# Where in 256 bytes the split operands of a fused attention and feed-forward kernel begin: one place per chunk for x, one per slot for the squares

## The chip, the cores and the metric

The kernel runs on one core of a Trainium2 chip, as one program. The metric is the device time of the whole program in microseconds, smaller is better. The time before is 639.32 us, the median of three runs (634.35, 640.18 and 639.32 us); one more execution was taken with the hardware profiler and lasted 636.35 us, of which the span from the first to the last instruction is 634.6 us.

## The reference, cut to what matters

Attention over 4 batches, 8 heads, 768 positions and 64 values per head: each query sees the keys less than 16 positions away, and 24 summaries of blocks of 32 (the maximum of the keys, the mean of the values). The result, 3072 tokens of 512 values, goes through a feed-forward layer with squared ReLU.

```python
    k_sum = k.reshape(B, H, nb, block, D).max(axis=3)
    v_sum = v.reshape(B, H, nb, block, D).mean(axis=3)
    scores_all = np.concatenate([scores_l_m, scores_s], axis=-1)   # window, then summaries
    a = np.exp(scores_all - max); a = a / (a.sum() + 1e-09)
    x = np.matmul(a, v_all)                       # -> (3072, 512)
    h = np.maximum(x @ w_in, 0.0)                 # 512 -> 2048
    return h * h @ w_out                          # 2048 -> 512
```

## The kernel before, in words

**Numbers.** Everything that TensorE multiplies in the feed-forward layer is split into a high part and a low part of four bytes per value (type fp32r): x into `xh` and `xl`, the weights into two halves of `w_sb[f]`, the squares into `gh` and `gl`. Each product is then three matmuls: high by high, high by low, low by high.

**Chunks, blocks and slots.** The 3072 tokens are 12 chunks of 256 (`c`), the 2048 hidden values are 16 blocks of 128 (`f`). The first layer, `ffn1` (L391, matmuls at L395), makes one block of one chunk from 12 matmuls: for each of four parts of the 512 inputs, the stationary operand is 128x128 of `w_sb[f]`, and the moving operand is 256 columns (1024 bytes per partition) of `xh` or `xl`. The second layer, `ffn2` (L429, matmuls at L436), makes for each of the two halves of the chunk three matmuls with a stationary 128x128 piece of `gh` or `gl` and a moving operand of 512 columns of `w_sb[f]`. A slot (L470) handles two blocks: 24 matmuls of the first layer, then 12 matmuls of the second layer for the two blocks of the slot before, and then ScalarE and VectorE make this slot's squares (`squares`, L420: ReLU at L403, high square L409, exact square L414, low part L417). In the text, F1 is the group of 24 matmuls and F2 the group of 12; a chunk is eight slots, so eight times F1 and F2.

**The order.** The first two chunks and the attention ahead of them (groups 0 to 5) are written out by hand in the string `START` (L43), because the weights arrive and are split there. From chunk 2 on (L641) the slots run in order, and `period` (L487) hangs the attention of later groups between them: in the eighth slot's place stand `outputs` (L354, matmuls at L364), `scores_by_group` (L269, matmuls at L281) and `split_x` (L384), which writes `xh` (L379, ScalarE) and `xl` (L382, VectorE) of the next chunk. The program's order is the one written; no planner changes it.

**Places.** All tiles of interest are in the SBUF, each partition's bytes one after the other. In the built program the weights' rooms (pool `big`, 8192 bytes each) all begin at byte 160 of a 256-byte line of addresses, and so do the buffers of x and of the squares. All pieces of the weights that a matmul reads begin at multiples of 512 bytes in their room, all pieces of x at multiples of 512 behind the first byte of the chunk's x. So the difference between where x begins and where the weights begin, taken in 256 bytes, is just the number that the list `begin_x` (L110) gives for that chunk: one number for `xh`, one for `xl`. In this document "place" is this number, taken in 256. `x_buf` has two buffers for each of `xh` and `xl`, each with 128 values to spare, and `x_part` (L374) takes buffer `c % 2` from `begin_x[c]` on. Chunks 0 to 11 have the places 0, 0, 0, 64, 128, 192, 256 (which is 0), 32, then (`xh`, `xl`) = (0, 64), (0, 128), (0, 256), and 320 (which is 64). The squares `gh_sb` and `gl_sb` (L113, L114) are one tile each, of four blocks of 1024 bytes; a slot uses two of them, the next slot the other two. Their place is always 0.

Of the kernel before, what the change touches and what calls it, by code (L numbers as in the profile page):

```python
# [12 lines left out]
F32R = mybir.dt.float32r  # L13
# [11 lines left out]
P = 128  # L25
NT = S // P
NPAIR = H // 2
TPC = 2
CT = TPC * P
# [44 lines left out]
def attn_ffn_kernel(ctx: ExitStack, tc: tile.TileContext, q, k, k0, kt, v, vt, v0, w, masks, gmasks, ident, mean, out):  # L74
# [3 lines left out]
    const = ctx.enter_context(tc.tile_pool(name="const", bufs=1))  # L78
# [28 lines left out]
    ksum = const.tile([P, NPAIR, NB], F32, name="ksum")  # L107
    vsum = const.tile([P, NPAIR, 32], F32, name="vsum")

    begin_x = [(0, 0), (0, 0), (0, 0), (64, 64), (128, 128), (192, 192), (256, 256), (32, 32), (0, 64), (0, 128), (0, 256), (320, 320)]  # L110
    x_buf = {n: [const.tile([P, NPAIR * CT + 128], F32R, name=f"{n}{i}") for i in range(2)] for n in ("xh", "xl")}
    r_sb = const.tile([P, 2, CT], F32, name="r")
    gh_sb = const.tile([P, 4, CT], F32R, name="gh")  # L113
    gl_sb = const.tile([P, 4, CT], F32R, name="gl")  # L114


    bank = [ps_s.tile([P, DM], F32, name=n, tag=f"{n}{i}") for i, n in enumerate(["s_ps"] * 4 + ["ph"] * 2)]
# [26 lines left out]
    def sum_v0(vn):  # L144


        ps = ps_o.tile([P, DM], F32, name="o_ps")
        for t in range(NT):
            o = 20 - 4 * t
            for j in range(4):  # L150
                nc.tensor.matmul(
                    ps[j * 32 : j * 32 + 32, 0:P], lhsT=mean_sb[:, o : o + 32],
                    rhs=vn[t // 3][:, t % 3, j * P : (j + 1) * P], start=(t == 0), stop=(t == NT - 1),
                )
        return ps

    def place_v0(ps, j, eng):
        for g in range(2):
            copy(
                eng, v_sb[g][96:128, :, j * P : (j + 1) * P],  # L160
                ps[j * 32 : j * 32 + 32, 0:P].unsqueeze(1).to_broadcast([32, 2, P]),
            )
# [18 lines left out]
    def sum_k(b, p):  # L181
        nc.vector.tensor_reduce(
            out=ksum[:, p], in_=kv[b, p][:, 0:S].rearrange("a (n j) -> a n j", j=BLOCK), op=ALU.max, axis=AX.X
        )

    def sum_v(b, p):
        nc.vector.tensor_reduce(
            out=vsum[:, p, 0:NB], in_=kv[b, p][:, S : 2 * S].rearrange("a (n j) -> a n j", j=BLOCK), op=ALU.add, axis=AX.X
        )
        nc.vector.tensor_scalar_mul(vsum[:, p, 0:NB], vsum[:, p, 0:NB], 1.0 / BLOCK)  # L190

    def place_k(g):
        dst = by_run(g)[:, 4] if g < FROM_GROUPS else by_pair(g)[:, :, :, 64:GK]
        nc.vector.tensor_copy(out=dst, in_=ksum.unsqueeze(1).to_broadcast([P, 2, NPAIR, NB]))
# [58 lines left out]
    xh, xl = {}, {}  # L253
# [60 lines left out]
    def exponentials(g, h):  # L314
        half, i = divmod(h, 4)
        e = e_sb[:, h, 0 : NK if g < FROM_GROUPS else GK]
        nc.scalar.activation(e, e, AF.Exp, bias=nmx[half][:, i : i + 1], scale=-1.0, accum_out=sm[half][:, i : i + 1])  # L317
# [7 lines left out]
    def inverse(half):  # L325
        nc.vector.tensor_scalar_add(sm[half], sm[half], 1.0e-9)  # L326
        nc.vector.reciprocal(sm[half], sm[half])  # L327
        del nmx[half]
# [49 lines left out]
    def high_x(g):  # L378
        nc.scalar.copy(out=x_part(xh, "xh", g), in_=x_ps[g])  # L379
# [11 lines left out]
    def ffn1(c, f, ph):  # L391
        n = 0
        for cc in range(NC4):
            for w, x in ((0, xh), (1, xh), (0, xl)):
                nc.tensor.matmul(  # L395
                    ph, lhsT=w_sb[f][:, w, cc * P : (cc + 1) * P], rhs=x[c][:, cc, :], start=(n == 0), stop=(n == 3 * NC4 - 1)
                )
                n += 1
        return ph

    def relu(ph, r, eng):
        if eng is nc.scalar:
            nc.scalar.activation(r, ph, AF.Relu)  # L403
        else:
            eng.tensor_scalar_max(r, ph, 0.0)  # L405
        return r

    def high_square(gh, r):
        nc.scalar.activation(gh, r, AF.Square)  # L409
        return gh  # L410

    def square(ph, r):

        nc.vector.tensor_mul(out=ph, in0=ph, in1=r)  # L414

    def low_square(gl, ph, gh):
        nc.vector.tensor_sub(out=gl, in0=ph, in1=gh.bitcast(F32))  # L417
        return gl

    def squares(ph, k):  # L420

        r = relu(ph, r_sb.rearrange("p a b -> p (a b)"), nc.scalar)
        gh, gl = (b[:, 2 * k : 2 * k + 2, :].rearrange("p a b -> p (a b)") for b in (gh_sb, gl_sb))
        high_square(gh, r)
        square(ph, r)
        low_square(gl, ph, gh)
        return [(gh_sb[:, 2 * k + i, :], gl_sb[:, 2 * k + i, :]) for i in range(2)]

    def ffn2(c, f, gh, gl, first, last):  # L429
        if first:  # L430
# [11 lines left out]
    def evict(c, f, tt, eng):  # L442

        if (c, tt) in parked:
            ob = parked[c, tt]
            nc.vector.tensor_add(out=ob, in0=o_ps[c][tt], in1=ob)
        else:
            ob = work.tile([P, DM], F32, name="ob", tag="ob", bufs=4)
            copy(eng, ob, o_ps[c][tt])
        if f < NF - 1:  # L450
            parked[c, tt] = ob
        else:
            r0 = c * CT + tt * P
            nc.sync.dma_start(out=out[r0 : r0 + P, :], in_=ob)
# [7 lines left out]
    def finish():  # L462

        for p in behind:
            ffn2(*p)
        done = [p[:2] for p in behind if p[-1]]
        behind.clear()
        return done[0] if done else None

    def slot(c, f, before, after, last):  # L470

        ph = bank[4 + f // 2 % 2]
        for i in range(2):
            ffn1(c, f + i, ph[:, i * CT : (i + 1) * CT])
        done = finish()
        for do in before:
            do()
        for i, g_ in enumerate(squares(ph, f // 2 % 2)):
            behind.append((c, f + i, *g_, f + i == 0, f + i == NF - 1))
        for tt in range(2 if done else 0):  # L480
            evict(*done, tt, nc.scalar)
        for do in after:
            do()
        for do in last:
            do()
# [45 lines left out]
    vn, tp, ph_of, r_of, g_of, v_mean = {}, {}, {}, {}, {}, {}  # L531
# [30 lines left out]
    def begin(op, i, j, eng):  # L562


        if op == "KS":
            sum_k(0, i)
        elif op == "PK":
            place_k(i)
        elif op == "SV":
            v_mean[0] = sum_v0([vn[0], vn[1]])  # L570
        elif op == "VC":
            place_v0(v_mean[0], i, eng)
        elif op == "KT":
            sum_k(1, i)
        elif op == "VT":
            sum_v(1, i)

        elif op == "S":
            if i < FROM_GROUPS:
                (scores_kt if i < FROM_KT else scores)(i, 2 * j, 2 * j + 2)  # L580
            else:
                scores_by_group(i)
        elif op == "TT":
            mask_max(i, j)
        elif op == "E":
            exponentials(i, j)
        elif op == "NR":
            inverse(j)
        elif op == "N":
            norm(i, j, eng)  # L590
        elif op == "T":
            held["T", i, j] = free.pop(0)
            tp[i, j] = turn_pe(i, j, bank[held["T", i, j]])
        elif op == "TC":
            copy(eng, pT[i % 2][:, j * 4 : j * 4 + 4], tp.pop((i, j)))
            free.append(held.pop(("T", i, j)))
        elif op == "O":
            outputs(i)
        elif op == "XH":
            high_x(i)  # L600
        elif op == "XL":
            low_x(i)

        elif op in ("HI", "LO", "SH", "AD", "CA", "SU"):
            {"HI": sign_w, "LO": round_w, "SH": shift_w, "AD": add_w, "CA": high_w, "SU": low_w}[op](i, eng)

        elif op == "F1":
            held["F1", i] = free.pop(0)
            ph_of[i] = ffn1(*units[i][:2], bank[held["F1", i]][:, 0:CT])
        elif op == "RE":  # L610
            r_of[i] = relu(ph_of[i], r_sb[:, i % 2, :], eng)
        elif op == "SQ":
            g_of[i] = [high_square(gh_sb[:, i % 4, :], r_of[i])]
        elif op == "MU":
            square(ph_of[i], r_of[i])
        elif op == "GL":
            g_of[i].append(low_square(gl_sb[:, i % 4, :], ph_of.pop(i), g_of[i][0]))
            free.append(held.pop(("F1", i)))
        elif op == "F2":
            c, f, f0, f1 = units[i]  # L620
            ffn2(c, f, *g_of.pop(i), f == f0, f == f1 - 1)
        elif op == "EV":
            evict(*units[[4, 15, 26, 31][i]][:2], j, eng)
        else:
            raise AssertionError(op)

    with tc.manual_schedule(engines=None):
        for token in START.split():
            what, i, j, eng = re.fullmatch(r"(L:[a-z]+|F[12]|[A-Z]+)\.?(\d*)\.?(\d*)([avp]?)", token).groups()
            i, j = int(i or 0), int(j or 0)  # L630
# [10 lines left out]
        for c in range(2, n_c):  # L641
            for f in range(0, NF, 2):
                n = (f + 2) // 2 % 8
# [85 lines left out]
```

## Time and profile before

| what | value |
|---|---|
| median of three runs | 639.32 us |
| the profiled execution | 636.35 us |
| its span | 634.6 us |
| mean granted TensorE clock | 0.989 |
| TensorE matmul busy | 605.5 us, 95% |
| TensorE weight load busy | 546.8 us, 86% |
| VectorE, ScalarE, GpSimd busy | 386.1, 262.7 and 88.3 us |
| chain that ended last: matmuls of L395 and of L436 | 44% and 41% |

The chain of work that ended last is followed back from the last instruction; each of its rows has the start, the length, the engine, what it writes, the line and the number of instructions. A matmul's own duration in the profile (283 ns for 256 columns) is longer than the step from one matmul's start to the next, since matmuls are pipelined. What counts for the time is the step; it is the length of a row of the chain divided by its count.

### The profile page before, as it was taken

How to read it: one execution, taken by the hardware profiler on the slowest of the kernel's cores; microseconds unless marked ns; L12 is line 12 of the kernel's file. 1: busy time of each engine (PE TensorE's matmuls, PEld its weight loads, DVE VectorE, ACT ScalarE, POOL GpSimd, SP SyncE). 2: the span in 40 equal slices, each digit the busy share in tenths (PEclk: the TensorE clock that was granted, in tenths of full speed). 3: DMA queues.
4: the chain of work that ended last, by engine and by line, in shares of the span. 5: the costliest groups of instructions: out<-in, count | busy, mean ns of one | idle time of the engine just before them, and what ended most of it. 6: DMA issues, size and time to landing. Idle time of an engine off the chain costs nothing.

```text
span 634.6 us, 14142 instructions
## 1 busy us (share of the span) xinstructions
PE 605.5 (95%) x5792; PEld 546.8 (86%) x5792; DVE 386.1 (61%) x1077; ACT 262.7 (41%) x690; POOL 88.3 (14%) x83
## 2 busy tenths in 40 slices
PE   3699999999989999999999998999999999999997
PEld 2488889989979989999989987998998998998996
DVE  4889989768535755756644772683763663653221
ACT  3678887232424324424424423333424333332222
POOL 2565662002000000002000000000200000000000
PEclk9879999999999999999999998999999999999999
DMA  9999611553043134124016106205005001000000
GB/s 302 364 344 323 210 62 52 165 171 81 1 110 110 48 86 132 51 70 99 1 53 165 51 26 159 84 1 135 35 1 135 34 0 52 34 2 1 34 1 33
DMA packets 55105, 60.56 MB, mean 95 GB/s; under 512 B 40321, under 2 KB 40449, under 8 KB 52993
## 3 DMA queue, kind: packets, MB, share of 16 engines
q1 hardware_dynamic: 55040, 59.67, 31.5%
q8 instruction: 45, 0.74, 0.5%
q14 instruction: 20, 0.16, 0.1%
HBM read 53.36 MB, written 6.29 MB: 94 GB/s over the span
## 4 chain that ended last, share of the span: by engine, by line
PE 93%; DMA 3%; DVE 2%; issue 1%; SPq 0%; ACT 0%; DVEq 0%
PE ph L395 41%; PE o_ps L436 41%; PE ph L364 3%; PE s_ps L395 3%; PE s_ps L281 2%; DMA q_sb<-in_q 2%; PE s_ps L296 1%; DMA mask_sb<-in_masks 1%; DVE e_sb L309 1%; PE s_ps L364 1%; PE ph L339 1%; PE s_ps L264 0%; DVE sm L326 0%; SPq L174 0%; DVE w_raw L239 0%
## 5 line engine op out<-in xcount | busy, mean ns | idle before, releaser
L395 PE MATMUL ph<-xh,w_sb 128*128 128x256 f32 x1448 | 265.3, 283 | 2.6 <-issue 2.1
L395 PEld LDWEIGHTS ph<-xh,w_sb 128*128 128x128 f32 x1448 | 230.0, 191 | 10.8 <-issue 2.6
L436 PE MATMUL o_ps<-w_sb,gh 128*128 128x512 f32 x768 | 238.8, 392 | 0.0
L395 PE MATMUL ph<-xl,w_sb 128*128 128x256 f32 x724 | 204.5, 282 | 0.0
L414 DVE TENSOR_TENSOR ph<-ph,r 128x512 f32<-128x512 f32 (+1 forms) x101 | 64.8, 643 | 162.8 <-ACT r L403 162.1
L436 PEld LDWEIGHTS o_ps<-w_sb,gh 128*128 128x128 f32 x768 | 137.6, 188 | 23.8 <-issue 0.2
L436 PE MATMUL o_ps<-w_sb,gl 128*128 128x512 f32 x384 | 150.0, 390 | 0.8 <-DVE gl L417 0.8
L403 ACT ACTIVATE r<-ph 128x512 f32<-128x512 f32 (+1 forms) x91 | 51.8, 569 | 228.8 <-PE ph L395 223.3
L395 PEld LDWEIGHTS ph<-xl,w_sb 128*128 128x128 f32 x724 | 138.1, 191 | 0.0
L317 ACT ACTIVATE e_sb<-e_sb,nmx 128x88 f32<-128x88 f32 (+1 forms) x192 | 69.8, 365 | 69.9 <-DVE nmx L309 69.9
L350 DVE STREAM_TRANSPOSE pT<-e_sb 32x256 f32<-32x256 f32 x216 | 94.1, 435 | 3.4 <-POOL e_sb L333 0.4
L436 PEld LDWEIGHTS o_ps<-w_sb,gl 128*128 128x128 f32 x384 | 72.1, 188 | 17.3 <-DVE gl L417 1.3
L333 POOL TENSOR_TENSOR e_sb<-e_sb,sm 128x352 f32<-128x352 f32 (+1 forms) x43 | 34.6, 808 | 337.5 <-DVE sm L327 200.5
L417 DVE TENSOR_TENSOR gl<-ph,gh 128x512 fp32r<-128x512 f32 (+1 forms) x101 | 64.3, 636 | 10.6 <-DVE ph L414 0.5
L409 ACT ACTIVATE gh<-r 128x512 fp32r<-128x512 f32 (+1 forms) x112 | 63.9, 571 | 8.7 <-DVE r L405 5.2
L243 POOL TENSOR_TENSOR w_raw<-w_raw 128x1024 int32<-128x1024 int32 x16 | 35.2, 2210 | 27.2 <-DVE w_raw L239 10.1
L317 ACT ACTIVATION_READ_ACCUMULATOR e_sb<-e_sb,nmx 128x1 f32 x192 | 36.1, 188 | 0.0
L309 DVE CUSTOM_DVE_ANT_0 e_sb<-s_ps,gmask_sb 128x88 f32<-128x88 f32 x144 | 27.1, 245 | 0.4
L382 DVE TENSOR_TENSOR xl<-ph,xh 128x512 fp32r<-128x512 f32 x19 | 13.1, 691 | 22.7 <-ACT xh L379 22.7
L326 DVE TENSOR_SCALAR sm<-sm 128x4 f32<-128x4 f32 x48 | 13.5, 281 | 16.2 <-ACT e_sb L317 16.2
L379 ACT CAST xh<-ph 128x512 fp32r<-128x512 f32 x19 | 11.1, 586 | 26.9 <-PE ph L364 26.9
L364 PEld LDWEIGHTS ph<-pT,v_sb 128*64 128x64 f32 x608 | 18.6, 138 | 3.8 <-issue 3.2
(66 smaller groups left out, 391.7 us busy)
## 6 DMA issues: line engine op xcount, KB each, us to landing
w_raw<-in_w SPq DMA_DIRECT2D x16, 1024.0 KB, 14.6
v_sb<-in_v SPq DMA_DIRECT2D x24, 384.0 KB, 5.0
kv<-in_kt SPq DMA_DIRECT2D x16, 384.0 KB, 3.4
q_sb<-in_q SPq DMA_DIRECT2D x24, 256.0 KB, 5.4
out<-ob SPq DMA_DIRECT2D x24, 256.0 KB, 2.1
k_sb<-in_k SPq DMA_DIRECT2D x18, 256.0 KB, 5.2
kv<-in_vt SPq DMA_DIRECT2D x12, 384.0 KB, 3.9
k_sb<-in_k SPq DMA_DIRECT2D x18, 128.0 KB, 5.0
```

The source lines that it names most:

```text
L243: nc.gpsimd.tensor_tensor(out=hi, in0=hi, in1=lo, op=ALU.add)
L309: nc.vector.tensor_tensor_reduce(out=e_sb[:, h, 0:n], in0=s_ps[g][h % 2][:, h // 2, 0:n], in1=m, scale=-scale, scalar=3.0e38, op0=ALU.add, ...
L317: nc.scalar.activation(e, e, AF.Exp, bias=nmx[half][:, i : i + 1], scale=-1.0, accum_out=sm[half][:, i : i + 1])
L333: eng.tensor_mul(out=e, in0=e, in1=sm[half].unsqueeze(2).to_broadcast([P, 4, n]))
L350: nc.vector.transpose(out=pT[g % 2][j * 32 : j * 32 + 32, :, i * 32 : i * 32 + 32], in_=e_sb[i * 32 : i * 32 + 32, :, c : c + 32],)
L364: nc.tensor.matmul(xp[o : o + 64, h // 2, s * 64 : s * 64 + 64], lhsT=v_sb[g % 2][:, s, h * 64 : h * 64 + 64], rhs=pT[g % 2][:, h, s * 64 ...
L395: nc.tensor.matmul(ph, lhsT=w_sb[f][:, w, cc * P : (cc + 1) * P], rhs=x[c][:, cc, :], start=(n == 0), stop=(n == 3 * NC4 - 1))
L403: nc.scalar.activation(r, ph, AF.Relu)
L409: nc.scalar.activation(gh, r, AF.Square)
L414: nc.vector.tensor_mul(out=ph, in0=ph, in1=r)
L417: nc.vector.tensor_sub(out=gl, in0=ph, in1=gh.bitcast(F32))
L436: nc.tensor.matmul(o_ps[c][tt], lhsT=g_[:, ts_], rhs=w_sb[f][:, w, DM:], start=(first and n == 0), stop=(last and n == 2),)
```

## The change

The list `begin_x` gets other numbers: chunks 0 to 2 begin at place 192, chunks 3 to 9 at 196, 200, 208, 216, 224, 232 and 240, chunk 10 at 0 and chunk 11 at 64. `xh` and `xl` of a chunk now always have the same place. The x buffers are 64 values longer than the data instead of 128.

The squares get two buffers for each of `gh` and `gl`, one for each of two alternating slots, with 64 values to spare, and a list `begin_g` of eight places, one for each slot of a chunk: 0, 32, 64, 96, 128, 160, 192 and 16. `gh` and `gl` of a slot have the same place. In the hand-written beginning all squares are at place 0, as before.

```diff
-    begin_x = [(0, 0), (0, 0), (0, 0), (64, 64), (128, 128), (192, 192), (256, 256), (32, 32), (0, 64), (0, 128), (0, 256), (320, 320)]
-    x_buf = {n: [const.tile([P, NPAIR * CT + 128], F32R, name=f"{n}{i}") for i in range(2)] for n in ("xh", "xl")}
+    begin_x = [(192, 192), (192, 192), (192, 192), (196, 196), (200, 200), (208, 208), (216, 216), (224, 224), (232, 232), (240, 240), (0, 0), (64, 64)]
+    x_buf = {n: [const.tile([P, NPAIR * CT + 64], F32R, name=f"{n}{i}") for i in range(2)] for n in ("xh", "xl")}
     r_sb = const.tile([P, 2, CT], F32, name="r")
-    gh_sb = const.tile([P, 4, CT], F32R, name="gh")
-    gl_sb = const.tile([P, 4, CT], F32R, name="gl")
+    begin_g = [(0, 0), (32, 32), (64, 64), (96, 96), (128, 128), (160, 160), (192, 192), (16, 16)]
+    g_buf = {n: [const.tile([P, 2 * CT + 64], F32R, name=f"{n}{i}") for i in range(2)] for n in ("gh", "gl")}
+    def squares_of(k, f):
+        return [
+            g_buf[n][k][:, o // 4 : o // 4 + 2 * CT].rearrange("p (a b) -> p a b", a=2)
+            for n, o in zip(("gh", "gl"), begin_g[f // 2 % len(begin_g)])
+        ]
...
-    def squares(ph, k):
+    def squares(ph, k, f):
         r = relu(ph, r_sb.rearrange("p a b -> p (a b)"), nc.scalar)
-        gh, gl = (b[:, 2 * k : 2 * k + 2, :].rearrange("p a b -> p (a b)") for b in (gh_sb, gl_sb))
+        both = squares_of(k, f)
+        gh, gl = (b.rearrange("p a b -> p (a b)") for b in both)
         high_square(gh, r)
         square(ph, r)
         low_square(gl, ph, gh)
-        return [(gh_sb[:, 2 * k + i, :], gl_sb[:, 2 * k + i, :]) for i in range(2)]
+        return [(both[0][:, i, :], both[1][:, i, :]) for i in range(2)]
...
-        for i, g_ in enumerate(squares(ph, f // 2 % 2)):
+        for i, g_ in enumerate(squares(ph, f // 2 % 2, f)):
...
-            g_of[i] = [high_square(gh_sb[:, i % 4, :], r_of[i])]
+            g_of[i] = [high_square(squares_of(i // 2 % 2, 0)[0][:, i % 2, :], r_of[i])]
...
-            g_of[i].append(low_square(gl_sb[:, i % 4, :], ph_of.pop(i), g_of[i][0]))
+            g_of[i].append(low_square(squares_of(i // 2 % 2, 0)[1][:, i % 2, :], ph_of.pop(i), g_of[i][0]))
```

In the built program every engine has the same instructions in the same order and with the same waits as before. The addresses that differ are those of `xh` and `xl`, of `r` (moved by 1024 bytes) and of the squares; the two kinds of buffers together take the same 26,624 bytes per partition, so everything behind them, the weights' rooms too, stays where it was. All these buffers still begin at byte 160 of 256, so the numbers in the two lists are the places, as before.

## The prediction

> **What bounds the kernel now.** I read the page first: its busy times and the chain that ended last.
>
> ```profile
> PE 605.5 (95%) x5792; PEld 546.8 (86%) x5792; DVE 386.1 (61%) x1077; ACT 262.7 (41%) x690; POOL 88.3 (14%) x83
> PE 93%; DMA 3%; DVE 2%; issue 1%; SPq 0%; ACT 0%; DVEq 0%
> L395 PE MATMUL ph<-xh,w_sb 128*128 128x256 f32 x1448 | 265.3, 283 | 2.6 <-issue 2.1
> L436 PE MATMUL o_ps<-w_sb,gh 128*128 128x512 f32 x768 | 238.8, 392 | 0.0
> ```
>
> TensorE sets the end: 93% of the chain is its own work, and its two large groups hardly ever wait. So the change can act only through the step from one matmul to the next. The second view cuts out, for each of the chunks 2 to 11, seven slots without the attention's matmuls (seven times F1 and F2). The first number behind the window is its length, then come the engines' busy times, the granted clock, the DMA share and the rate.
>
> ```profile
> core 0: us, PE busy (x) PEld busy (x) DVE busy (x) ACT busy (x) POOL busy (x), PEclk, DMA share, GB/s
> 140.08:179.61 39.53, 39.53 (x257) 35.82 (x253) 26.62 (x80) 14.30 (x46) 4.78 (x7) 1.00 0.20 51
> 191.22:230.41 39.19, 39.19 (x253) 35.37 (x251) 27.49 (x80) 15.47 (x48) 3.09 (x4) 1.00 0.19 61
> 239.59:279.17 39.58, 39.58 (x254) 35.71 (x252) 27.91 (x82) 15.38 (x48) 3.09 (x4) 1.00 0.23 69
> 288.45:327.37 38.92, 38.92 (x253) 35.36 (x251) 25.20 (x78) 15.60 (x48) 4.78 (x7) 1.00 0.12 31
> 337.59:377.03 39.44, 39.44 (x254) 35.72 (x252) 27.53 (x80) 15.51 (x48) 3.09 (x4) 1.00 0.19 59
> 390.73:429.65 38.92, 38.92 (x253) 35.19 (x251) 27.92 (x82) 15.46 (x48) 3.10 (x4) 1.00 0.12 42
> 438.95:478.06 39.11, 39.11 (x254) 35.36 (x252) 25.15 (x78) 15.56 (x48) 4.78 (x7) 1.00 0.10 25
> 487.35:526.27 38.92, 38.92 (x254) 35.36 (x252) 23.59 (x74) 15.47 (x48) 3.09 (x4) 1.00 0.10 26
> 535.76:575.19 39.43, 39.43 (x253) 35.72 (x251) 23.61 (x74) 15.49 (x48) 3.09 (x4) 1.00 0.04 14
> 583.48:622.59 39.11, 39.11 (x254) 35.57 (x252) 9.74 (x14) 9.78 (x16) 0.00 (x0) 1.00 0.04 14
> ```
>
> In each window TensorE is busy from end to end at clock 1.00, with the same matmuls, yet the lengths go from 38.92 to 39.58 us. They go with the place: 39.53 and 39.44 for place 0 (chunks 2 and 6), 39.58 for 128, 39.19 and 39.11 for 64, 38.92 for 192 and for 32. VectorE's load doesn't order them (27.92 us in one of the fastest, 23.61 in a slow one), nor does the DMA share (0.04 in a slow one). Where x begins is worth up to 1.7% here. Its two groups, from the chain in order of time (start, length, work):
>
> ```profile
> 108.83 2.88 PE ph L395 x24
> 168.44 2.87 PE ph L395 x24
> 171.31 2.75 PE o_ps L436 x12
> 219.31 2.83 PE ph L395 x24
> 222.14 2.76 PE o_ps L436 x12
> 256.68 2.88 PE ph L395 x24
> 259.55 2.76 PE o_ps L436 x12
> 310.80 2.83 PE ph L395 x24
> 313.63 2.72 PE o_ps L436 x12
> 407.54 2.80 PE ph L395 x24
> 410.34 2.75 PE o_ps L436 x12
> ```
>
> By place, F1 takes 2.87 (0), 2.83 (64), 2.88 (128), 2.83 (192) and 2.80 us (32): 116.7 to 120 ns a matmul. F2 takes 2.72 to 2.76 us, and 2.72 is 226.7 ns a matmul. There is one F1 that is faster than all these, the last of chunk 3, which comes behind the attention's matmuls; rows of its low part (every third matmul), then two of the next F1:
>
> ```profile
> 234.36 0.28 PE L395 MATMUL ph<-xl,w_sb 128*128 128x256 f32 x1
> 236.74 0.28 PE L395 MATMUL ph<-xl,w_sb 128*128 128x256 f32 x1
> 239.83 0.28 PE L395 MATMUL ph<-xl,w_sb 128*128 128x256 f32 x1
> 240.19 0.28 PE L395 MATMUL ph<-xl,w_sb 128*128 128x256 f32 x1
> ```
>
> From 234.36 to 236.74 lie 21 matmuls: 113.3 ns each, half of F2's 226.7 for half as many columns. Behind it, at place 128, three matmuls take 0.36 us, 120 each. So I read 113.3 and 226.7 ns as the pace without disturbance, and the rest, 0 to 6.7 ns a matmul, as what the weight load of the next matmul costs the reading of this one when both meet in the same part of the 256 bytes. It depends on the place, and a little on how a group was entered, since the same place 64 gave 113.3 once and 117.9 in the other slots.
>
> **The change part by part.** No instruction, wait or DMA is added or moved, so everything goes by steps.
>
> *x of chunks 2 to 11.* F1 before, mean over the ten chunks (2.87, 2.83, 2.88, 2.83, 2.87, 2.80, 2.83, 2.83, 2.87, 2.83; the three with two places take 2.83, 2.83 and 2.87 by their windows): 2.844 us. After: chunk 2 at 192 has 2.83, chunk 10 at 0 has 2.87, chunk 11 at 64 has 2.83, all from rows. The seven places from 196 to 240 are in no row. Bounds: undisturbed 24 x 113.3 ns = 2.72, and the worst seen, 2.88. The nearest rows are 192 (2.83) just below them and 32 (2.80), which, like 224, is an odd multiple of 32; I take the middle, 2.815. Mean after: (2.83 + 7 x 2.815 + 2.87 + 2.83) / 10 = 2.8235. Over 80 slots: -0.0205 x 80 = **-1.6 us**; with the seven at 2.72 or at 2.88 it would be -6.9 or +2.0.
>
> *x of chunks 0 and 1*, from place 0 to 192. These are 384 matmuls that go from 120 ns (the row at 108.83) to 117.9: at most -0.8 us. Since TensorE also waits for other things in this stretch, I take half, **-0.4 us**.
>
> *The squares' place in F2*, other than 0 in seven of eight slots, 70 of the 80. Here the weight load reads the squares while w streams past. No row has another place than 0. There F2 starts disturbed and then settles: 2.746 us on average against 2.72 undisturbed. Bounds: 2.72, so -0.026 x 70 = -1.8 us; and a disturbance in each matmul as large as F1's largest, 2.72 + 12 x 6.7 ns = 2.80, so +0.054 x 70 = +3.8 us. I take a little above today's, 0.01, because place 0 is one that settles and others need not: **+0.7 us**.
>
> *Writing.* ScalarE and VectorE now write x and the squares to other places. What hides it: in the windows above, ScalarE is busy 16 of 39 us and VectorE at most 28, and a slot's squares are needed one whole F1 later. Only the `split_x` ahead of the last chunk has no cover, since no attention is left that could stand between:
>
> ```profile
> 576.39 0.59 ACT xh L379
> 577.01 0.70 DVE xl L382
> ```
>
> That is 1.3 us, once; a tenth more would not be seen, so nothing for it. `r` and the second buffers move by whole multiples of 256 bytes: nothing.
>
> The sum is -1.6 - 0.4 + 0.7 = -1.3 us, against the profiled execution's own 636.35: 635.05. That execution has two stalls of its own, with a slow piece behind the second:
>
> ```profile
> 183.85 2.11 issue
> 380.67 2.62 issue
> 383.80 4.36 PE ph L395 x24
> ```
>
> Over 2 us each, and 1.5 us for the F1 behind the second (4.36 against the 2.87 of its place). How many of these a run has explains how the runs can lie between 634.35 and 640.18; the change doesn't touch them. The four executions shown have a mean of 637.55, 1.2 above the profiled one and 1.8 below the median of the three, so I forecast **636.2 us**.
>
> [...]
>
> **The rivals.**
>
> *The undisturbed pace spreads.* A square at another place changes the phase in which F2 hands over to F1, and F1 then finds the 113.3 ns of the row at 234.36. For it: that row, at a place that otherwise gives 117.9. Against: the other F1 that come behind the attention's matmuls, and so in another phase too, settle at their place's usual pace. If it happens in the 70 slots with a moved square, F1 gains (2.844 - 2.72) x 70 = 8.7 us, with the 0.4 of the beginning 9.1: from 637.55 to 628.4 us.
>
> *The squares collide.* From another place than 0 the load of the squares meets the stream of w in every matmul and F2 doesn't settle. It can be dearer than the 6.7 ns above, since a matmul of F2 has twice the columns and can be met twice: at 13.3 ns F2 is 2.88 us, +0.134 x 70 = +9.4, less the 2.0 for x: 645.0 us, slower by over 1%. It decides from an F2 of about 2.87 on. For it: F1 is disturbed at every place seen. Against: F2 settles today, having twice the time for each load.
>
> *Starts that are no multiple of 16 bytes* (196, 200, 216, 232; every row before is at a multiple of 32) cost a disturbance more per matmul: 4 chunks x 192 x 6.7 ns = 5.1 us on top of the forecast: 641.3 us. Nothing in the trace speaks for or against it. [...]
>
> **How the numbers follow.** The forecast, a mix of places with F1 at 2.80 to 2.83 on average and F2 near today's, has 0.68; the undisturbed pace 0.16; colliding squares 0.07; the 16-byte starts 0.09. A measurement of this kernel tells about 1%, 6.4 us, from no change. Faster by more than that comes from the undisturbed pace (0.14 of its 0.16) and the forecast's edge (0.03): 0.17. Slower comes from colliding squares (0.06) and the edge (0.01): 0.07. Within 1%: 0.76. The range goes from 628, near the first rival, to 642, which holds the third and the spread of the runs.
>
> **What would show it.** Right: windows of seven slots between 38.7 and 39.4 us for chunks 3 to 9, chunk 10 near 39.4, chunk 11 near 39.1, F1 rows of 2.80 to 2.83, F2 rows of 2.72 to 2.80 that differ from slot to slot with a period of eight. Wrong: F1 rows of 2.72 in many slots; F2 rows of 2.87 or more; chunks 3, 4, 6 and 8 slower than 5, 7 and 9; or all windows alike, whatever the place.

## The result, and the profile after

The changed kernel takes 640.35 us, the median of 18 runs (636.91 to 643.01), against 636.76 us for the kernel before in 18 runs (634.35 to 640.18). The ratio is 1.0046, 95% interval 1.0025 to 1.0068: slower by 2.9 us (1.6 to 4.3). The forecast was a change of -1.3 us. The profiled execution of the changed kernel has a span of 638.9 us, 4.3 more than before.

The page of the changed kernel shows the same picture as before, with TensorE's two groups a little dearer per matmul (L404 and L446 are the former L395 and L436):

```profile
PE 609.3 (95%) x5792; PEld 547.9 (86%) x5792; DVE 386.6 (61%) x1077; ACT 263.0 (41%) x690; POOL 88.5 (14%) x83
L404 PE MATMUL ph<-xh,w_sb 128*128 128x256 f32 x1448 | 267.0, 285 | 2.8 <-issue 2.0
L446 PE MATMUL o_ps<-w_sb,gh 128*128 128x512 f32 x768 | 240.5, 394 | 0.0
```

No new wait has come in, and ScalarE, VectorE and GpSimd do the same work in the same time. The whole difference lies in the steps. The windows of seven slots for chunks 2 to 11, as shown of the kernel before (length, busy times of the engines, clock, DMA share, rate):

```profile
139.81:178.98 39.17, 39.17 (x257) 35.23 (x252) 26.63 (x80) 14.33 (x46) 4.79 (x7) 1.00 0.20 51
190.33:230.13 39.80, 39.80 (x253) 35.82 (x252) 27.49 (x80) 15.49 (x48) 3.10 (x4) 1.00 0.16 55
239.48:279.33 39.85, 39.85 (x253) 35.82 (x252) 27.90 (x82) 15.43 (x48) 3.10 (x4) 1.00 0.20 63
288.67:328.17 39.50, 39.50 (x253) 35.48 (x251) 25.19 (x78) 15.59 (x48) 4.79 (x7) 1.00 0.10 29
338.67:378.68 40.01, 40.01 (x253) 35.99 (x251) 27.48 (x80) 15.48 (x48) 3.10 (x4) 1.00 0.19 60
392.54:432.03 39.49, 39.49 (x254) 35.51 (x252) 27.88 (x82) 15.48 (x48) 3.10 (x4) 1.00 0.11 41
441.32:481.15 39.83, 39.83 (x254) 35.83 (x252) 25.20 (x78) 15.60 (x48) 4.79 (x7) 1.00 0.10 28
490.51:529.83 39.32, 39.32 (x253) 35.33 (x252) 23.58 (x74) 15.47 (x48) 3.10 (x4) 1.00 0.10 29
539.61:579.29 39.68, 39.68 (x253) 35.69 (x252) 23.61 (x74) 15.49 (x48) 3.10 (x4) 1.00 0.04 14
587.57:626.85 39.28, 39.28 (x254) 35.57 (x253) 9.74 (x14) 9.80 (x16) 0.00 (x0) 1.00 0.04 14
sum 395.93, PE 395.93 PEld 356.25 DVE 244.70 ACT 148.14 POOL 32.99; mean PE 39.59 PEld 35.63 DVE 24.47 ACT 14.81 POOL 3.30
```

Their sum is 395.93 us; the ten windows of before add up to 392.15. That is +3.78 us in 70 of the 80 slots, +4.3 for all, and the beginning is 0.3 shorter (chunk 2 begins at 139.81 instead of 140.08). Chunks 10 and 11 tell the two parts apart at once: their x is at 0 and at 64, which took 39.44 and 39.11 to 39.19 us before, and now they take 39.68 and 39.28. That is what the squares' places cost. The chain of chunk 3 (x at 196) shows both groups; each F2 belongs to the slot before, and from the second one on the squares' places are 0, 32, 64, 96 and 128:

```profile
193.38 2.79 PE o_ps L446 x12
196.16 2.88 PE ph L404 x24
199.05 2.74 PE o_ps L446 x12
201.79 2.89 PE ph L404 x24
204.68 2.79 PE o_ps L446 x12
207.47 2.88 PE ph L404 x24
210.36 2.80 PE o_ps L446 x12
213.16 2.88 PE ph L404 x24
216.04 2.81 PE o_ps L446 x12
218.85 2.88 PE ph L404 x24
221.73 2.78 PE o_ps L446 x12
```

F1 is at 2.88 where 2.80 to 2.83 was forecast, and F2 returns to 2.74 only with the squares at 0. Counted over the trace, from the first matmul of a group to the first of the next one (the last F2 ahead of the attention without the 0.09 to 0.10 us of the change to the attention's matmuls):

| place of x | 192 | 196 | 200 | 208 | 216 | 224 | 232 | 240 | 0 | 64 |
|---|---|---|---|---|---|---|---|---|---|---|
| F1 after, us | 2.805 | 2.883 | 2.884 | 2.840 | 2.912 | 2.840 | 2.886 | 2.816 | 2.868 | 2.828 |

| place of the squares | 0 | 32 | 64 | 96 | 128 | 160 | 192 | 16 |
|---|---|---|---|---|---|---|---|---|
| F2 after, us | 2.737 | 2.800 | 2.800 | 2.804 | 2.785 | 2.80 | 2.758 | 2.792 |

F1 has a mean of 2.856 against 2.845 before, F2 2.783 against 2.744: +0.9 and +3.1 us over 80 slots. These are means: at 208, F1 takes 2.80 us behind the squares at 16 and 96 and 2.85 to 2.86 behind the others.

### The profile page after: what moved, and what is told of

Its sections match the earlier page's. It is cut to its first block, busy times and chain, and to the rows that moved or that the text cites. A ratio compares the mean times of both kernels' runs of the same rounds, so it can differ in the third digit from the quotient of the medians.

```text
span 638.9 us, 14142 instructions
## 1 busy us (share of the span) xinstructions
PE 609.3 (95%) x5792; PEld 547.9 (86%) x5792; DVE 386.6 (61%) x1077; ACT 263.0 (41%) x690; POOL 88.5 (14%) x83
## 4 chain that ended last, share of the span: by engine, by line
PE 91%; DVE 3%; DMA 3%; ACT 2%; issue 1%; SPq 0%; DVEq 0%; ACTq 0%
PE o_ps L446 40%; PE ph L404 40%; PE ph L373 3%; PE s_ps L290 2%; PE s_ps L404 2%; DMA q_sb<-in_q 2%; DMA mask_sb<-in_masks 1%; PE s_ps L305 1%; DVE w_sb L259 1%; PE ph L348 1%; PE s_ps L373 1%; ACT e_sb L326 0%; DVE e_sb L318 0%; PE s_ps L273 0%; ACT w_sb L133 0%
## 5 line engine op out<-in xcount | busy, mean ns | idle before, releaser
L404 PE MATMUL ph<-xh,w_sb 128*128 128x256 f32 x1448 | 267.0, 285 | 2.8 <-issue 2.0
L404 PEld LDWEIGHTS ph<-xh,w_sb 128*128 128x128 f32 x1448 | 230.8, 191 | 11.5 <-issue 2.2
L446 PE MATMUL o_ps<-w_sb,gh 128*128 128x512 f32 x768 | 240.5, 394 | 0.0
L404 PE MATMUL ph<-xl,w_sb 128*128 128x256 f32 x724 | 205.1, 283 | 0.0
L446 PEld LDWEIGHTS o_ps<-w_sb,gh 128*128 128x128 f32 x768 | 137.7, 188 | 25.3 <-issue 0.2
L446 PE MATMUL o_ps<-w_sb,gl 128*128 128x512 f32 x384 | 151.3, 394 | 0.9 <-DVE gl L426 0.9
L404 PEld LDWEIGHTS ph<-xl,w_sb 128*128 128x128 f32 x724 | 138.6, 191 | 0.0
L446 PEld LDWEIGHTS o_ps<-w_sb,gl 128*128 128x128 f32 x384 | 72.1, 188 | 17.9 <-DVE gl L426 1.3
```

The source lines that it names most:

```text
L404: nc.tensor.matmul(ph, lhsT=w_sb[f][:, w, cc * P : (cc + 1) * P], rhs=x[c][:, cc, :], start=(n == 0), stop=(n == 3 * NC4 - 1))
L446: nc.tensor.matmul(o_ps[c][tt], lhsT=g_[:, ts_], rhs=w_sb[f][:, w, DM:], start=(first and n == 0), stop=(last and n == 2),)
```

## The experiments

**Each part alone, and two plain versions.** The theory after the result: each group's pace is set by its own operand's place, and the two parts add up. The main rival: the squares' place acts on F1 through the handover from F2. These four were timed beside the kernel before.

First, x as in the change, all squares back at 0:

```diff
-    begin_g = [(0, 0), (32, 32), (64, 64), (96, 96), (128, 128), (160, 160), (192, 192), (16, 16)]
+    begin_g = [(0, 0)] * 8
```

> The changed kernel with every square back at place 0; x keeps its new places. Theory of places: each group's pace is set by its own operand's place. Then F1 stays as in the changed kernel (2.88 us a group at 196, 200 and 232, 2.91 at 216, 2.82 to 2.85 at 208, 224 and 240), and F2 returns to 2.72 to 2.76 us; against before F1 costs +0.013 x 80 = +1.0 us, the hand-written beginning gives back some 0.4: ratio about 1.001. Rival, the handover: F1 at these places is slow because the F2 ahead of it ends in another phase. Then F1 falls to the forecast 2.80 to 2.83 us, and the ratio is 0.997.

Measured: ratio 1.0024 (0.9994 to 1.0055), in itself not clear of no change. The windows of chunks 3, 4 and 6 (x at 196, 200 and 216):

```profile
189.74:229.31 39.57, 39.57 (x254) 35.81 (x252) 27.49 (x80) 15.51 (x48) 3.10 (x4) 1.00 0.16 55
238.62:278.05 39.43, 39.43 (x254) 35.81 (x252) 27.94 (x82) 15.42 (x48) 3.10 (x4) 1.00 0.22 69
...
336.72:376.29 39.57, 39.57 (x254) 35.95 (x252) 27.50 (x80) 15.51 (x48) 3.10 (x4) 1.00 0.20 61
```

F1 stays at 2.889, 2.885 and 2.911 us with the squares at 0, now the same to 0.001 in each slot, and F2 is back at 2.73 to 2.77. So x's own place makes F1 slow at 196, 200, 216 and 232 (2.887). The handover rival, which would have F1 at 2.80 to 2.83 here, falls for these places.

Second, the squares as in the change, x as before (256 and 320 are written as 0 and 64, which are the same places):

```diff
+    begin_x = [(0, 0), (0, 0), (0, 0), (64, 64), (128, 128), (192, 192), (0, 0), (32, 32), (0, 64), (0, 128), (0, 0), (64, 64)]
```

> The x places of before, the squares' places of the change. Theory of places: F2 takes 2.78 us on average (2.80 at 16, 32, 64, 96 and 160, 2.78 at 128, 2.75 at 192, 2.74 at 0), F1 stays as before (2.80 us at 32, 2.83 at 64 and 192, 2.87 at 0): +0.038 x 80 = +3.1 us, ratio 1.0048. Rival, the handover: the moved squares raise F1 as well, by 0.03 us at each place, another +2.4 us, ratio 1.0086. Second rival, F2 is slow only beside x at starts that are no multiple of 16 bytes: F2 as before, ratio 1.000.

Measured: ratio 1.0041 (1.0015 to 1.0067). F2 has a mean of 2.782 us, F1 2.839, not raised but 0.006 lower than before. This part alone is slower, and it is the larger part; the two parts' +2.6 and +1.5 us add up to the whole within their intervals. Where F1 is lower, the handover shows after all. The chain of chunk 5, x at 192:

```profile
291.92 2.75 PE ph L404 x24
294.67 2.79 PE o_ps L446 x12
297.46 2.83 PE ph L404 x24
300.29 2.76 PE o_ps L446 x12
303.05 2.83 PE ph L404 x24
305.88 2.81 PE o_ps L446 x12
308.69 2.83 PE ph L404 x24
311.52 2.80 PE o_ps L446 x12
314.32 2.75 PE ph L404 x24
317.07 2.79 PE o_ps L446 x12
319.86 2.83 PE ph L404 x24
322.69 2.78 PE o_ps L446 x12
325.47 2.73 PE ph L404 x24
```

With the same x, F1 takes 2.83 us behind most F2, but 2.75, 2.75 and 2.73 behind those with squares at 192, 64 and 128. So a pace near the undisturbed one that a single row of the kernel before had shown can come from the squares' place, in this run at x 192 alone; at 128, F1 falls from 2.88 to between 2.84 and 2.85 behind some squares, and at 32 it hardly moves (2.80 to 2.81).

Third and fourth, one place for all x, and all squares at 0:

```diff
+    begin_x = [(32, 32)] * 12      # the other: (192, 192)
+    begin_g = [(0, 0)] * 8
```

> x of all chunks at place 32, all squares at 0. Theory of places: F1 2.80 us in every chunk, F2 2.74: 5.547 a slot against 5.589 before, -0.042 x 80 = -3.4 us, and up to -1.3 us in the hand-written beginning: ratio 0.993 to 0.995. Rival, what a chunk's F1 takes has to do with where the chunk stands in the run and not with the place: 5.589 a slot, ratio 1.000.

> x of all chunks at place 192, all squares at 0. Theory of places: F1 2.83 us, F2 settled at once, 2.72: 5.547 a slot as with place 32, ratio 0.993 to 0.996, although F1 and F2 share it out otherwise. Rival, F2's settling does not depend on x's place: F2 2.745, 5.572 a slot, ratio 0.997 to 0.998.

Measured: 0.9966 (0.9943 to 0.9988) for 32, 0.9942 (0.9917 to 0.9966) for 192. In each, every chunk takes the same: F1 2.803 and F2 2.744 with 32, F1 2.827 and F2 2.720 with 192 (slots behind the attention apart, which take longer). The squares are at 0 in both, so F2's pace depends on x's place too, as the theory had it for 192. Two chunks of the latter, far apart in the run, one beside a busy VectorE and one beside an idle one:

```profile
240.45:279.37 38.92, 38.92 (x254) 35.37 (x252) 27.92 (x82) 15.40 (x48) 3.10 (x4) 1.00 0.24 72
...
583.75:622.58 38.83, 38.83 (x254) 35.55 (x253) 9.75 (x14) 9.81 (x16) 0.00 (x0) 1.00 0.04 14
```

So a chunk's pace has to do with its place and not with where it stands or what the other engines do. (The last window is 0.09 shorter, since no attention follows it.)

**Pairs.** One pair of places per chunk, the squares' list now read by the chunk (as in all four scans below):

```diff
-            for n, o in zip(("gh", "gl"), begin_g[f // 2 % len(begin_g)])
+            for n, o in zip(("gh", "gl"), begin_g[f % len(begin_g)])
...
-        for i, g_ in enumerate(squares(ph, f // 2 % 2, f)):
+        for i, g_ in enumerate(squares(ph, f // 2 % 2, c)):
```

> One pair of places (x, squares) for each chunk from 2 to 11, the squares' place now by chunk and the same in all its slots: (192,192), (192,64), (192,128), (64,192), (64,64), (32,192), (32,64), (0,192), (224,192), (192,0). In the run with the squares alone, F1 at x 192 fell from 2.83 to 2.73 to 2.75 us behind an F2 with squares at 64, 128 or 192. Theory of places with a handover at x 192: these three pairs hold F1 at 2.73 to 2.75 us in all slots, (192,192) with F2 at 2.75, 5.50 a slot against 5.547 for (192,0); the other x places keep their F1 (2.83 at 64, 2.80 at 32, 2.87 at 0, 2.84 at 224). Rival, places alone: F1 is 2.83 us at 192 whatever the squares, 5.57 a slot for (192,192).

Measured: my theory of the handover failed in its simple form. (192,192) settles at F1 2.827 and F2 2.767; (192,64) and (192,128) alternate from slot to slot, 2.74 and 2.83, 2.73 and 2.83; the others keep their F1 within 0.01 (2.82 to 2.83 at 64, 2.806 and 2.800 at 32, 2.878 at 0, 2.842 at 224). So F1 at 192 isn't set by the two places alone, but also by the state in which the slot ahead leaves it. Rows of the chain of chunk 4, (192,128):

```profile
251.35 2.83 PE ph L404 x24
254.18 2.78 PE o_ps L446 x12
256.95 2.73 PE ph L404 x24
```

**A scan of x,** squares at 0:

```diff
+    begin_x = [...] + [(a, a) for a in (16, 48, 80, 96, 112, 144, 160, 176, 8, 4)]
```

> Squares at 0; x of chunks 2 to 11 at 16, 48, 80, 96, 112, 144, 160, 176, 8 and 4. Theory of start within 16 bytes: only 8 and 4 give F1 of 2.88 to 2.91 us, the other eight 2.80 to 2.86. Rival, distance from the weights' place: the F1 near 0 (4, 8, 16) are as slow as at 0, 2.87, and 200, 216 and 232 were slow by their distance; then 80, 96 and 112 show no order by multiples of 16 either. F2 2.72 to 2.77 us everywhere.

Measured, F1 in us: 16: 2.850, 48: 2.846, 80: 2.867, 96: 2.882, 112: 2.758, 144: 2.800, 160: 2.854, 176: 2.853, 8: 2.880, 4: 2.940. Starts at 8 and 4 are slow, as the first theory had it; but 96 is as slow as 8, and 112 is far below all that were forecast. Distance to 0 gives no order either. The windows of 96, 112, 144 and 4:

```profile
288.02:327.64 39.62, 39.62 (x254) 35.76 (x252) 25.18 (x78) 15.58 (x48) 4.78 (x7) 1.00 0.09 26
338.19:376.82 38.63, 38.63 (x253) 34.89 (x251) 27.51 (x80) 15.38 (x48) 3.09 (x4) 1.00 0.19 59
389.26:427.99 38.73, 38.73 (x253) 35.18 (x252) 27.93 (x82) 15.42 (x48) 3.09 (x4) 1.00 0.17 57
...
583.29:623.28 39.99, 39.99 (x253) 36.37 (x252) 9.74 (x14) 9.79 (x16) 0.00 (x0) 1.00 0.04 14
```

**A scan of the squares,** x at 192:

```diff
+    begin_g = [...] + [(a, a) for a in (224, 208, 240, 48, 80, 112, 8)] + [(0, 32), (32, 0), (32, 32)]
```

> x at 192; squares of chunks 2 to 8 at 224, 208, 240, 48, 80, 112 and 8, then gh and gl apart: (gh, gl) = (0, 32), (32, 0), and (32, 32). Theory that each load of squares meets the stream of w by its own place: F2 2.79 to 2.81 us at all of the first seven (8 perhaps more), and (0, 32), with one of three loads moved, adds a third of (32, 32)'s rise over 2.72, (32, 0) two thirds: 2.75, 2.77 and 2.80. Rival, the disturbance comes from jumping between places: (0, 32) and (32, 0) as slow as (32, 32) or slower.

Measured, F2 in the later slots: 224: 2.798, 208: 2.779, 240: 2.745, 48: 2.801, 80: 2.778, 112: 2.786, 8: 2.768; then (0,32): 2.788, (32,0): 2.771 and 2.793 in turn, (32,32): 2.793. Five of the seven are lower than I expected, and the loads don't add up one by one: moving `gl` alone, a third of the loads, already brings 0.068 of the 0.073 us. That is nearer to the rival. With the squares at 8, F1 was 2.725 in every slot, but so had the chunk ahead been (112: 2.727).

**The weights moved.** Is it the place in 256 bytes that counts, or the distance to the weights?

```diff
+    const.tile([P, 16], F32, name="pad")
```

> 64 bytes of padding ahead of the weights' rooms, so that the weights begin 64 later in 256; x numbers 0, 64, 96, 128, 192 and 32 with squares' number 64 for chunks 2 to 7, then x 0 with squares 0, 96, 128 and 192. Theory that only the distance to the weights counts: F1 takes what it took at places 192, 0, 32, 64, 128 and 224, so 2.83, 2.87, 2.80, 2.83, 2.88 and 2.84 us, with F2 2.72 to 2.77 in these six; then F2 as at squares' places 192, 32, 64 and 128, so 2.75, 2.80, 2.80 and 2.78. Rival, the place in 256 bytes itself counts: F1 2.87, 2.83, unknown, 2.88, 2.83 and 2.80, F2 2.80 in the first six, then 2.74 at 0.

Measured: F1 2.826, 2.872, 2.802, 2.830, 2.876 and 2.839 us in the first six chunks, F2 2.720 to 2.767; then F2 2.767, 2.794, 2.788 and 2.800 in turn, 2.776. These are, to 0.001 or 0.002 us, the values that the pairs with 64 less have elsewhere, down to the alternation of (192,64); only (192,192) has 2.767 instead of my 2.75, as in the run of pairs. Windows of x numbers 0, 64, 96, 128 and 192:

```profile
140.36:179.26 38.90, 38.90 (x258) 35.32 (x253) 26.63 (x80) 14.33 (x46) 4.78 (x7) 1.00 0.21 52
192.22:231.66 39.44, 39.44 (x254) 35.74 (x252) 27.51 (x80) 15.48 (x48) 3.10 (x4) 1.00 0.13 45
240.99:279.91 38.92, 38.92 (x253) 35.22 (x252) 27.92 (x82) 15.35 (x48) 3.09 (x4) 1.00 0.22 69
289.20:328.40 39.20, 39.20 (x254) 35.40 (x252) 25.16 (x78) 15.55 (x48) 4.78 (x7) 1.00 0.10 27
338.77:378.34 39.57, 39.57 (x253) 35.73 (x251) 27.49 (x80) 15.48 (x48) 3.09 (x4) 1.00 0.21 64
```

Number 0 is fast here and 64 slow, the other way round than before. The distance between the two operands counts, and the rival is out. Whole multiples of 256 don't count: in the kernel before, 256 takes what 0 takes (2.873 and 2.872 us), and 320 what 64 takes (2.830 both).

**Versions that beat both kernels,** and a finer scan. All x at 112 with squares at 0; all x at 192 with squares at 8; pairs by chunk.

```diff
+    begin_x = [(112, 112)] * 12    # the other: (192, 192)
+    begin_g = [(0, 0)] * 8         # the other: (8, 8)
```

> All x at 112, all squares at 0. Theory of places: as in chunk 6 of the scan of x, F1 2.758 and F2 2.749 us in every slot, 5.507 against 5.589 before: -0.082 x 80 = -6.6 us, and up to -2 in the hand-written beginning: ratio 0.987 to 0.990. Rival, the 2.758 was a phase that the chunk ahead of it happened to hand on: F1 at 2.85 like its neighbours at 80 and 144 with multiples of 16, 5.60 a slot, ratio 1.000.

> All x at 192, all squares at 8. Theory of places with the handover: F1 2.725 and F2 2.768 us as in chunk 8 of the scan of squares, 5.493 a slot: -0.096 x 80 = -7.7 us and up to -2 in the beginning: ratio 0.985 to 0.989. Rival, the handover has more than one lasting state and chunk 8 inherited the fast one from the chunk ahead, whose F1 was 2.727 already: then F1 is 2.83 us in many chunks, 5.595 a slot, ratio 1.000.

> Pairs (x, squares) by chunk: (112,8), (144,8), (160,8), then squares 0 with x at 104, 120, 108, 116, 136 and 152, then (192,4). Theory of places: F1 with squares at 8 stays near what it has at 0 (2.76, 2.80, 2.85), F2 rises to 2.77 and more; x at 108 and 116, odd multiples of 4, give 2.88 to 2.94 like 196 and 4, and 104, 120, 136, 152, odd multiples of 8, 2.88 to 2.91 like 8, 200, 216 and 232. Rival, it is the distance to 112 that counts: then 104 to 120 all lie near 2.76 to 2.80.

Measured: 628.29 us, ratio 0.9875 (0.9856 to 0.9895), for 112 and 0; 626.63 us, ratio 0.9842 (0.9824 to 0.9861), for 192 and 8, both beside a median of 637.27 before. The fast state of (192,8) is a lasting one: chunk 2 comes from another state and reaches it at its third slot. Windows of chunks 2, 3 and 10 of that version:

```profile
137.87:176.65 38.78, 38.78 (x257) 34.90 (x252) 26.67 (x80) 14.33 (x46) 4.79 (x7) 1.00 0.20 50
189.54:228.11 38.57, 38.57 (x253) 34.70 (x251) 27.20 (x76) 15.09 (x47) 3.10 (x4) 1.00 0.14 50
...
526.87:565.42 38.55, 38.55 (x254) 34.68 (x252) 23.59 (x74) 15.48 (x48) 3.10 (x4) 1.00 0.04 15
```

The mean window falls from 39.22 to 38.57, that is 7.4 us over 80 slots. Chunk 2 begins 2.2 us sooner; how much of this is the beginning's share is not shown, since its start differs as much between profiles with the same places in the beginning (138.32 to 140.27 us in seven of them).

The finer scan spoils any simple rule. F1 with squares at 0: 104: 3.088, 108: 2.872, 116: 2.922, 120: 2.903, 136: 2.874, 152: 2.876 us. Nearness to 112, the rival, is out with that. The window of 104:

```profile
287.95:328.66 40.71, 40.71 (x253) 36.98 (x252) 25.16 (x78) 15.64 (x48) 4.78 (x7) 1.00 0.10 27
```

With squares at 8, 112 has 2.800 and 144 about 2.846 instead of 2.758 and 2.800, against what I expected; (192,4) alternates between 2.73 and 2.83.

## Why the prediction was wrong

The time after lies within the forecast's range of 628 to 642 us, but the change has the wrong sign: +2.9 us, clear of none, where -1.3 was forecast.

*What bounds the kernel* was right: no wait, clock or other engine enters the difference between the windows; they moved by the steps of F1 and F2 alone, and the reading of 113.3 and 226.7 ns as the undisturbed pace holds. In no lasting state here is F1 below 2.72 us, and the best (2.725) is 113.5 ns a matmul.

*The squares' place in F2* is the step that failed most. The prediction took "a little above today's", +0.7 us of a span from -1.8 to +3.8. Measured: F2 with moved squares has a mean of 2.791 us against 2.745, +3.2 us over 70 slots, not far from the upper bound. The reason given, that place 0 settles and others need not, was right; the size was not. The upper bound, a disturbance in each matmul as large as F1's largest, was the better guide: five of the seven moved places have 2.79 to 2.80 us.

*x of chunks 2 to 11* had the wrong sign. The seven places without a row were set to 2.815 us, between their neighbours 192 and 32; they take 2.866 on average. Of this, the four that are no multiple of 16 take 2.891, +2.4 us over 32 slots, and the other three 2.832, +0.4; chunk 2 at 192 gave back 0.2 by the handover. So -1.6 became +0.9 us. Interpolating between neighbours was the error: the pace is no smooth function of the place (96 has 2.882, 104 3.088, 108 2.872, 112 2.758). The bound of 2.88 was too low as well; 216 has 2.91. (The term's lower bound, -6.9, comes to -7.0 from the same rows.)

*The hand-written beginning* ended 0.3 us sooner, near the 0.4 forecast, but that is no proof: between profiles with the same places there, it ends up to 2 us apart. Its rows of F1 fell from 2.87 to 2.83, as forecast. *Writing* cost nothing (`xh` and `xl` ahead of the last chunk take 0.59 and 0.70 us again), and *no instruction moved* held.

*The stalls* are in both profiles (1.99 and 2.69 us after) and don't enter the difference. The slow F1 behind the second one has to do with the clock: 4.36 us at a mean granted clock of 0.66 (383 to 388 us) before, 4.53 at 0.66 (385 to 390 us) after, but 2.95 at 1.00 behind a stall of 2.67 us in the run with x at 112. All thirteen profiles have both stalls (the second 1.00 us long in one and 2.62 to 2.95 in the others), but only eight the slow F1. So runs differ by this dip of the clock rather than by the number of stalls; how much of their spread it makes is open.

*The rivals.* The 16-byte starts, which had 0.09, were a guess that no row of before showed, and they are about half true. The sign named for them came: chunks 3, 4, 6 and 8 take 39.80 to 40.01 us a window, 5, 7 and 9 take 39.32 to 39.50. But no run shows the 5.1 us named for them: the four chunks lose 2.4 us against the forecast. Every place tried that is no multiple of 16 takes 2.87 us or more with squares at 0 (twelve places, 2.87 to 3.09, mean 2.91), the sixteen multiples 2.76 to 2.88, mean 2.84. But 0, 96 and 128 are multiples of 16 and take 2.872, 2.882 and 2.875 us, so this is not the main thing. A pace near the undisturbed one (2.73 and 2.75 us) came in two slots of chunk 2, not in 70. Colliding squares came at the single price of 2.80, not at the 2.88 that would have decided it. The sum of the terms as measured, 3.1 + 0.9 - 0.3 = +3.7 us (the last of them not resolved), fits the +4.3 of the spans and the interval of 1.6 to 4.3.

*What stays open.* That the weight load of the next matmul costs the stream of this one when both meet is my reading, from the distance between the two operands (with the weights moved by 64 bytes, F1 takes 2.826 us at number 0 and 2.872 at 64); no run here separates the two accesses, so it is argued and not shown. Why 112 is fast and 104 the slowest, and which pairs alternate, I can't say from these runs.

## What to carry to other kernels

Where TensorE is busy from end to end, compare its step per matmul with the fastest step anywhere in the trace; if it differs between pieces with the same shapes (here F1 has 113.5 to 128.7 ns a matmul), look early at where the operands begin relative to each other. Here the effect could not be interpolated (F1 takes 2.872 us at 108, 2.758 at 112 and 2.922 at 116): measure each pair of places, many in one run by giving each chunk its own, and then run the best pair throughout, since a group's pace also depended here on the state the group ahead left (F1 2.73 and 2.83 us in turn at x 192 with squares at 128). A list that mixes places is for finding out; for the time, one good pair in all slots (here x 192 with squares 8) took 1.6% off.

## What the runs showed of the hardware that was not expected

- The same seven slots of 36 matmuls each, all at clock 1.00 and with no waits, take from 38.55 us (x at 192, squares at 8) to 40.71 us (x at 104, squares at 0), with nothing changed but where x and the squares begin.
- Moving the weights by 64 bytes moves the pattern by 64, for all ten pairs tried: F1 2.83 us at number 0 and 2.87 at 64 instead of the reverse.
- The pace locks: a slot repeats to 0.001 us for whole chunks, some pairs alternate between two states (F1 2.73 and 2.83 at 192 with squares at 128), and one pair, (192,8), keeps F1, but for one or two slots behind the attention, within 0.005 us of the undisturbed 2.72.
